# An fp32 attention and two-MoE kernel on Trainium2: the first MoE's last pair in seven products, with low halves of its outputs for two token blocks on GpSimd

## The chip, the core and the metric

The kernel runs on one core of a Trainium2 chip. The metric is the time of one execution on the device in microseconds (us); the matrix engine is TensorE (PE), with PEld for its weight loads, and the others are VectorE (DVE), ScalarE (ACT), GpSimd (POOL) and SyncE (SP), which issues the DMAs.

## What is computed

Attention over 2 batches, 8 heads, 768 positions and head size 64, with a window of 128 and 4 sink positions; its output, as 1536 tokens of width 512, goes through two feed-forward blocks. Cut to what matters:

```python
x = attention(q, k, v).transpose(0, 2, 1, 3).reshape(1536, 512)
g = x @ w_gate                          # 512 x 1536
h = g * sigmoid(g) * (x @ w_val)        # w_val 512 x 1536
x = h @ w_out                           # first MoE, w_out 1536 x 512
h = x @ w_in                            # 512 x 2048
h = maximum(h, 0) + alpha * minimum(h, 0)
out = h @ w_out2                        # second MoE, 2048 x 512
```

All inputs and outputs are fp32.

## The kernel before

**Products.** An fp32 product is made of three on PE: each operand is split into a high half (rounded on ACT, `hh`, `yh`, `wh`) and a low half (operand minus high half, `hl`, `yl`, `wl`), and hi x hi, hi x lo and lo x hi are added up in PSUM. Each matmul is 128 x 128 by 128 x 512. `split_hidden` (L700) makes the two halves of a tile, the low half on DVE; `Stream` does it for weights, which arrive as 64-bit words: `w_m` on ACT (L556), three bit operations on DVE (L591, L594, L597), `wh` on ACT (L600) and `wl` on GpSimd (L606).

**Tiling.** The 1536 tokens are three blocks b = 0, 1, 2 of 512. Four tiles of 128 of the first MoE's inner width go first (`Moe1`), then four pairs of tiles, c = 0 to 3 (`Duo1`), then eight pairs of the second MoE (`Duo2`). A pair has a gate projection, a value projection and outputs. `proj` (L684) is one projection of one block and one tile: 12 matmuls (`ph`). An output (`output`, L1038) is six matmuls (`po`) for one of four column tiles m of one block, with an addition to the accumulator `acc` on DVE (L1048); for the last pair, which completes the first MoE, the sum is split as well (`yh`, `yl`), as the operand of the second MoE.

**Seven products.** Pairs c = 1 and 2, and those of the second MoE from its second on, compute the projections of blocks 0 and 1 in seven products of half size, not eight, in the manner of Strassen and Winograd (`Chain`, L879). Operands are the blocks' quarters (`xh`, `xl`), sums of them made once (`t1` to `t4`, each with halves h and l) and sums of weights (`SUMS`, L660; four 128x256 operations on GpSimd, L574 to L577, then `wh` at L580 and a `wl`). A product (`pa`, `pb`, `pc`, L858) is six matmuls. Products that several results share stay in PSUM and go on; ACT keeps a copy (`u1`, `u2`, L868) and DVE adds it to another product (`plus`, L885). Block 2 has no partner and goes by `proj`. `ORDER7` sets the order of the steps; in it the products with `t4` and `t3` have the numbers 4 and 7, the fourth quarter (`b22`) 3, and block 2's two projections 8 and 9. Pairs c = 0 and c = 3 are plain: each block by `proj`.

**From projections to outputs.** The gate's result goes through Silu on ACT to `sg`; the value's is multiplied with it on DVE (`hid`, L977), and the product is split: `hh` on ACT, `hl` on DVE. Index r is the tile in the pair. An output needs `hh` and `hl` of both.

**Order.** A unit is one pair as a Python generator. At the mark `OUT` its rest is held and run after the next unit's first step, so the next pair's first product stands between a pair's last value product and its outputs. In the plain last pair, blocks 0 and 1 have their outputs behind the next block's first projection and only block 2's are held. The order on each engine is then set by the framework's scheduler, which simulates the program and picks what is ready; what is written under `g.soon()` has priority. Weights go through raw tiles into slots: ten pairs of `wh` and `wl` in `w_p`, and two in `w_p3`, which `back` (L1267) opens when the room of `t3` is closed, here after pair 2's outputs; `st.own` names the weights that may use them.

Of the kernel before, what the change touches and what calls it, by code (L numbers as in the profile page):

```python
# [12 lines left out]
ALU = mybir.AluOpType  # L13
# [7 lines left out]
KD = DM // P  # L21
# [12 lines left out]
CHUNK = 4  # L34
DUO = 2
ORDER7 = (1, 2, 5, 6, 8, 7, 9, 4, 3)
WB = 10
RB = 3
# [460 lines left out]
def big(g, name, parts=(0, 1)):  # L499

    return [half(g.x_p, name) if j in parts else None for j in range(2)]
# [161 lines left out]
def duo1_seq(wg, wv, wo):  # L663

    seq = []
    for f in range(CHUNK, NF1, DUO):
        fs = range(f, f + DUO)
        more = SUMS if CHUNK < f < NF1 - DUO else []
        seq += [(0, wg, x, DOWN, x) for x in fs] + more
        seq += [(0, wv, x, DOWN, NF1 + x) for x in fs] + more  # L670
        seq += [(1, wo, x, DOWN, 2 * NF1 + x) for x in fs]
    return seq
# [26 lines left out]

def split_hidden(nc, hid, hh, hl):  # L700
    nc.scalar.activation(hh, hid, AF.Copy)  # L701
    nc.vector.tensor_tensor(out=hl, in0=hid, in1=hh, op=ALU.subtract)  # L702

# [228 lines left out]
class Duo1(Duo):  # L932
# [48 lines left out]

    def plain(self, w, last):

        pairs, ys = {}, {}
        _, gate, _, value = self.sinks(pairs)
# [11 lines left out]

        def second(b):
            y = [big(self.g, n) for n in ("yh", "yl")] if last else None
            for m in range(KD):  # L1000
                self.output(b, m, w + 2 * DUO, *pairs[b], y)
                yield
            if last:
                self.accs[b][1][1] += 1
                self.put(y, self.accs[b][0])

        yield from first(0, 0, gate)
        for b in range(NPASS):
            if b < NPASS - 1:
                yield from first(b, DUO, value)  # L1010
                yield from first(b + 1, 0, gate)
                yield from second(b)
        yield from first(b, DUO, value)
        yield OUT
        yield from second(b)
        self.st.done(DUO)

    def unit(self, c):
        last = (NF1 - CHUNK) // DUO - 1
        w = self.base + (3 * DUO + (c - 1) * 5 * DUO if c else 0)  # L1020
        if c in (0, last):
            yield from self.plain(w, c == last)
            return
        pairs = self.pairs()
        room_g, gate, room_v, value = self.sinks(pairs)
        for i, room, sink in ((0, room_g, gate), (2 * DUO, room_v, value)):
            chain = self.chain(w + i, self.ops, self.xs[2], room, sink)
            yield from chain.steps(ORDER7)
            chain.done()
        yield OUT  # L1030
        for b in (2, 0, 1):
            for m in range(KD):
                self.output(b, m, w + 4 * DUO, *pairs[b])
                yield
        self.st.done(DUO)

    def output(self, b, m, w, hh, hl, y=None):
# [9 lines left out]
        with self.g.soon():  # L1047
            nc.vector.tensor_tensor(out=av, in0=ps, in1=av, op=ALU.add)  # L1048
            if y:
                split_hidden(nc, av, *(chan(t, m) for t in y))  # L1050

# [109 lines left out]
def fast(nc, tc, ctx, g, lim, alpha, qk, vp, vs, w_gate, w_val, w_out, x2_in, x2_out, out):  # L1161
# [97 lines left out]
    inner = ExitStack()  # L1259
    last = (NF1 - CHUNK) // DUO - 1  # L1260

# [5 lines left out]
    def back():  # L1267
        assert not later
        inner.close()
        add_pool(nc, tc, ctx, g.w_ps, "w_p3", WA, "right")  # L1270
        st.own = range(base - 3 * DUO, len(st.seq))

    later.extend(x for y in d1.sums() for x in (None, y))
    units = [(m1.unit(0, 2), lend)] + [(d1.unit(c), back if c == last - 1 else None) for c in range(last + 1)]
    held = None
# [113 lines left out]
```

## Time and profile before

| | before |
|---|---|
| median of three runs | 667.65 us (667.52 to 668.27) |
| the profiled execution's own time | 667.32 us |
| its span, first to last instruction | 665.6 us |
| mean granted clock of TensorE | 0.983 of full speed |
| PE busy, matmuls | 646.0 us (97%), 3032 |
| DVE busy | 474.8 us (71%) |
| ACT busy | 319.8 us (48%) |
| GpSimd busy | 231.7 us (35%) |

How to read it: the profile is one execution, and its instructions have a start and a duration. Busy shares are means over stages. A matmul's row is 0.39 us long though a new one starts every 0.23 us, since matmuls are pipelined, so PE is counted by starts. In an answer on idle time, "a <- b" says that an engine waited before a for b. Tile names leave out the number of the buffer.

### The profile page before, as it was taken

How to read it: one execution, taken by the hardware profiler on the slowest of the kernel's cores; microseconds unless marked ns; L12 is line 12 of the kernel's file. 1: busy time of each engine (PE TensorE's matmuls, PEld its weight loads, DVE VectorE, ACT ScalarE, POOL GpSimd, SP SyncE). 2: the span in 40 equal slices, each digit the busy share in tenths (PEclk: the TensorE clock that was granted, in tenths of full speed). 3: DMA queues.
4: the chain of work that ended last, by engine and by line, in shares of the span. 5: the costliest groups of instructions: out<-in, count | busy, mean ns of one | idle time of the engine just before them, and what ended most of it. 6: DMA issues, size and time to landing. Idle time of an engine off the chain costs nothing.

```text
span 665.6 us, 8776 instructions
## 1 busy us (share of the span) xinstructions
PE 646.0 (97%) x3032; PEld 507.5 (76%) x3032; DVE 474.8 (71%) x933; ACT 319.8 (48%) x738; POOL 231.7 (35%) x259
## 2 busy tenths in 40 slices
PE   7889899999999999999999999999999999999996
PEld 3557566767788788888888888788888888888885
DVE  6897957355199736667898659858796889787554
ACT  4777755665364523452753345755334342524040
POOL 3557545334213532461333123424344252511000
PEclk8889799999999999999999999999999999999999
DMA  8764444100003303213432120212121303000005
GB/s 272 237 190 141 149 126 158 33 13 1 1 0 111 111 1 94 65 32 95 128 126 96 32 64 32 63 65 64 64 96 32 96 32 96 32 1 0 1 1 194
DMA packets 37204, 52.30 MB, mean 79 GB/s; under 512 B 4384, under 2 KB 28960, under 8 KB 37152
## 3 DMA queue, kind: packets, MB, share of 16 engines
q1 hardware_dynamic: 34944, 51.65, 24.4%
q8 instruction: 26, 0.43, 0.3%
q10 hardware_dynamic: 2208, 0.01, 0.2%
q14 instruction: 26, 0.21, 0.1%
HBM read 48.51 MB, written 3.15 MB: 78 GB/s over the span
## 4 chain that ended last, share of the span: by engine, by line
PE 81%; DVE 8%; ACT 4%; issue 2%; POOL 2%; DMA 1%; SPq 0%; ACTq 0%; POOLq 0%; DVEq 0%
PE pa L858 9%; PE pf L1133 7%; PE pf L1132 7%; PE pf L1131 7%; PE ph L688 6%; PE ph L690 6%; PE ph L689 6%; PE pb L858 4%; PE po L1043 3%; PE po L1044 3%; PE po L1045 3%; PE ps_s L227 3%; PE xp L323 2%; PE pc L858 2%; PE ps_p L282 2%
## 5 line engine op out<-in xcount | busy, mean ns | idle before, releaser
L606 POOL TENSOR_TENSOR wl<-w_m,wh 128x512 fp32r<-128x512 f32 x79 | 112.5, 1428 | 231.0 <-ACT wh L600 216.9
L600 ACT ACTIVATE wh<-w_m 128x512 fp32r<-128x512 f32 x68 | 43.0, 633 | 112.7 <-PE pf L1133 49.1
L701 ACT ACTIVATE hh<-hid 128x512 fp32r<-128x512 f32 x84 | 52.6, 630 | 72.5 <-DVE hid L977 29.7
L702 DVE TENSOR_TENSOR hl<-hid,hh 128x512 fp32r<-128x512 f32 x84 | 65.0, 778 | 16.9 <-ACT hh L701 16.5
L1132 PE MATMUL pf<-wl,hh 128*128 128x512 f32 x192 | 74.6, 392 | 0.0
L1131 PE MATMUL pf<-wh,hh 128*128 128x512 f32 x192 | 74.6, 392 | 0.0
L1138 DVE TENSOR_TENSOR acc<-pf,acc 128x512 f32<-128x512 f32 x84 | 54.6, 686 | 23.0 <-PE pf L1133 23.0
L1133 PE MATMUL pf<-wh,hl 128*128 128x512 f32 x192 | 68.9, 392 | 0.0
L556 ACT ACTIVATE w_m<-w_raw 128x512 f32<-128x512 f32 x68 | 45.9, 675 | 33.7 <-POOL wl L606 24.0
L597 DVE SCALAR_TENSOR_TENSOR w_m<-w_raw,w_m 128x512 uint32<-128x512 uint32 x68 | 58.6, 861 | 1.1
L594 DVE SCALAR_TENSOR_TENSOR w_m<-w_raw,w_m 128x512 int32<-128x512 int32 x68 | 52.3, 768 | 1.2
L688 PE MATMUL ph<-xh,wh 128*128 128x512 f32 x128 | 49.8, 389 | 0.0
L690 PE MATMUL ph<-xh,wl 128*128 128x512 f32 x128 | 49.8, 389 | 0.0
L689 PE MATMUL ph<-xl,wh 128*128 128x512 f32 x128 | 49.8, 389 | 0.0
L591 DVE TENSOR_SCALAR w_m<-w_m 128x512 int32<-128x512 int32 x68 | 36.7, 539 | 16.0 <-ACT w_m L556 15.4
L237 ACT ACTIVATE pr<-ps_s,nb 128x160 f32<-128x160 f32 (+2 forms) x96 | 38.1, 407 | 18.9 <-DVE nb L233 16.2
L1048 DVE TENSOR_TENSOR acc<-po,acc 128x512 f32<-128x512 f32 x48 | 31.8, 686 | 19.4 <-PE po L1045 19.3
L227 PE MATMUL ps_s<-th 64*128 64x288 f32 (+2 forms) x192 | 39.3, 443 | 6.0 <-ACT pr L237 4.5
L1132 PEld LDWEIGHTS pf<-wl,hh 128*128 128x128 f32 x192 | 36.1, 188 | 8.1
L1133 PEld LDWEIGHTS pf<-wh,hl 128*128 128x128 f32 x192 | 36.1, 188 | 8.0
L1131 PEld LDWEIGHTS pf<-wh,hh 128*128 128x128 f32 x192 | 36.1, 188 | 8.0
L1043 PE MATMUL po<-hh,wh 128*128 128x512 f32 x96 | 37.5, 391 | 0.6 <-ACT hh L701 0.6
(212 smaller groups left out, 1518.6 us busy)
## 6 DMA issues: line engine op xcount, KB each, us to landing
w_raw<-in_moe_w_out SPq DMA_DIRECT2D x28, 512.0 KB, 3.3
w_raw<-in_moe_w_in SPq DMA_DIRECT2D x16, 512.0 KB, 4.0
w_raw<-in_moe_w_gate SPq DMA_DIRECT2D x12, 512.0 KB, 4.0
w_raw<-in_moe_w_val SPq DMA_DIRECT2D x12, 512.0 KB, 3.7
th<-in_qk SPq DMA_DIRECT2D x16, 336.0 KB, 3.5
vr<-in_v SPq DMA_DIRECT2D x16, 192.0 KB, 2.9
out<-acc SPq DMA_DIRECT2D x12, 256.0 KB, 2.5
th<-in_qk SPq DMA_DIRECT2D x8, 256.0 KB, 5.4
```

The costliest lines, as they stand in the source:

```text
L227: nc.tensor.matmul(pss[e][:, :first + w], self.th[r, qs], self.th[r, ks], start=True, stop=True)
L597: nc.vector.scalar_tensor_tensor(out=mu, in0=lo.bitcast(U32), scalar=29, in1=mu, op0=ALU.logical_shift_right, op1=ALU.bitwise_or)
L606: eng.tensor_tensor(out=wl, in0=m, in1=wh, op=ALU.subtract)
L688: nc.tensor.matmul(ps, wh[:, c], chan(xh, kk), start=(kk == 0), stop=False)
L689: nc.tensor.matmul(ps, wh[:, c], chan(xl, kk), start=False, stop=False)
L690: nc.tensor.matmul(ps, wl[:, c], chan(xh, kk), start=False, stop=(kk == KD - 1))
L702: nc.vector.tensor_tensor(out=hl, in0=hid, in1=hh, op=ALU.subtract)
L858: self.nc.tensor.matmul(ps, a[:, c], m[:, k], start=(start and k == 0 and y == 0), stop=(k == 1 and y == 2), skip_group_check=True)
L1043: nc.tensor.matmul(ps, wh[:, mc], hh[:, x], start=(x == 0), stop=False)
L1131: nc.tensor.matmul(ps, hh[:, x, ts], wh, start=(x == 0), stop=False)
L1132: nc.tensor.matmul(ps, hh[:, x, ts], wl, start=False, stop=False)
L1133: nc.tensor.matmul(ps, hl[:, x, ts], wh, start=False, stop=(x == DUO - 1))
```

## The change

The last pair of the first MoE (c = 3) now goes in seven products too: its weights get the sums, and its value projection the order `LAST7`, in which the product with `t3` stands earlier and block 2's second projection last. Its outputs aren't held; they follow its value projection at once, in block order 0, 1, 2, and `OUT` stands behind them. `back` runs between the two, and only weights of the second MoE may use `w_p3`. Low halves of the pair's final sums for blocks 0 and 1 (8 of 128x512) are made on GpSimd; those of block 2 stay on DVE. `plain` is left for c = 0 alone.

```diff
--- before.py
+++ after.py
@@ -34,6 +34,7 @@
 CHUNK = 4
 DUO = 2
 ORDER7 = (1, 2, 5, 6, 8, 7, 9, 4, 3)
+LAST7 = (1, 2, 6, 5, 7, 8, 4, 3, 9)
 WB = 10
 RB = 3
 WA = 2
@@ -665,7 +666,7 @@
     seq = []
     for f in range(CHUNK, NF1, DUO):
         fs = range(f, f + DUO)
-        more = SUMS if CHUNK < f < NF1 - DUO else []
+        more = SUMS if f > CHUNK else []
         seq += [(0, wg, x, DOWN, x) for x in fs] + more
         seq += [(0, wv, x, DOWN, NF1 + x) for x in fs] + more
         seq += [(1, wo, x, DOWN, 2 * NF1 + x) for x in fs]
@@ -697,9 +698,9 @@
     return [(pool or g.h_p).tile([P, 2, T], F32R, tag=t, name=t) for t in ("hh", "hl")]
 
 
-def split_hidden(nc, hid, hh, hl):
+def split_hidden(nc, hid, hh, hl, eng=None):
     nc.scalar.activation(hh, hid, AF.Copy)
-    nc.vector.tensor_tensor(out=hl, in0=hid, in1=hh, op=ALU.subtract)
+    (eng or nc.vector).tensor_tensor(out=hl, in0=hid, in1=hh, op=ALU.subtract)
 
 
 class Moe1:
@@ -979,9 +980,9 @@
 
         return room_g, gate, room_v, value
 
-    def plain(self, w, last):
-
-        pairs, ys = {}, {}
+    def plain(self, w):
+
+        pairs = {}
         _, gate, _, value = self.sinks(pairs)
 
         def first(b, i, sink):
@@ -996,43 +997,47 @@
                 yield
 
         def second(b):
+            for m in range(KD):
+                self.output(b, m, w + 2 * DUO, *pairs[b])
+                yield
+
+        yield from first(0, 0, gate)
+        for b in range(NPASS - 1):
+            yield from first(b, DUO, value)
+            yield from first(b + 1, 0, gate)
+            yield from second(b)
+        yield from first(NPASS - 1, DUO, value)
+        yield OUT
+        yield from second(NPASS - 1)
+        self.st.done(DUO)
+
+    def unit(self, c):
+        last = c == (NF1 - CHUNK) // DUO - 1
+        if c == 0:
+            yield from self.plain(self.base)
+            return
+        w = self.base + 3 * DUO + (c - 1) * 5 * DUO
+        pairs = self.pairs()
+        room_g, gate, room_v, value = self.sinks(pairs)
+        for i, room, sink, order in ((0, room_g, gate, ORDER7), (2 * DUO, room_v, value, LAST7 if last else ORDER7)):
+            chain = self.chain(w + i, self.ops, self.xs[2], room, sink)
+            yield from chain.steps(order)
+            chain.done()
+        if last:
+            self.then()
+        else:
+            yield OUT
+        for b in (0, 1, 2) if last else (2, 0, 1):
             y = [big(self.g, n) for n in ("yh", "yl")] if last else None
             for m in range(KD):
-                self.output(b, m, w + 2 * DUO, *pairs[b], y)
+                self.output(b, m, w + 4 * DUO, *pairs[b], y)
                 yield
             if last:
                 self.accs[b][1][1] += 1
                 self.put(y, self.accs[b][0])
-
-        yield from first(0, 0, gate)
-        for b in range(NPASS):
-            if b < NPASS - 1:
-                yield from first(b, DUO, value)
-                yield from first(b + 1, 0, gate)
-                yield from second(b)
-        yield from first(b, DUO, value)
-        yield OUT
-        yield from second(b)
         self.st.done(DUO)
-
-    def unit(self, c):
-        last = (NF1 - CHUNK) // DUO - 1
-        w = self.base + (3 * DUO + (c - 1) * 5 * DUO if c else 0)
-        if c in (0, last):
-            yield from self.plain(w, c == last)
-            return
-        pairs = self.pairs()
-        room_g, gate, room_v, value = self.sinks(pairs)
-        for i, room, sink in ((0, room_g, gate), (2 * DUO, room_v, value)):
-            chain = self.chain(w + i, self.ops, self.xs[2], room, sink)
-            yield from chain.steps(ORDER7)
-            chain.done()
-        yield OUT
-        for b in (2, 0, 1):
-            for m in range(KD):
-                self.output(b, m, w + 4 * DUO, *pairs[b])
-                yield
-        self.st.done(DUO)
+        if last:
+            yield OUT
 
     def output(self, b, m, w, hh, hl, y=None):
         nc, st = self.nc, self.st
@@ -1047,7 +1052,7 @@
         with self.g.soon():
             nc.vector.tensor_tensor(out=av, in0=ps, in1=av, op=ALU.add)
             if y:
-                split_hidden(nc, av, *(chan(t, m) for t in y))
+                split_hidden(nc, av, *(chan(t, m) for t in y), eng=nc.gpsimd if b < NPASS - 1 else None)
 
 
 class Duo2(Duo):
@@ -1257,7 +1262,6 @@
                 decide(nc, g)
 
     inner = ExitStack()
-    last = (NF1 - CHUNK) // DUO - 1
 
     def lend():
         assert g.w_ps.pop()[1] == WA
@@ -1268,10 +1272,11 @@
         assert not later
         inner.close()
         add_pool(nc, tc, ctx, g.w_ps, "w_p3", WA, "right")
-        st.own = range(base - 3 * DUO, len(st.seq))
+        st.own = range(base, len(st.seq))
 
     later.extend(x for y in d1.sums() for x in (None, y))
-    units = [(m1.unit(0, 2), lend)] + [(d1.unit(c), back if c == last - 1 else None) for c in range(last + 1)]
+    d1.then = back
+    units = [(m1.unit(0, 2), lend)] + [(d1.unit(c), None) for c in range((NF1 - CHUNK) // DUO)]
     held = None
     for u, then in units + [(d2.unit(c, ys), None) for c in range(NF2 // DUO)]:
         for x in u:
```

In the order of the changed program lines stand one to five later than before (L858 is L859, L977 is L978, L1043 is L1048, L1048 is L1053). The number behind a tile's name is its buffer. PE has 3020 matmuls.

DVE before, where the plain last pair ends its block 0 and goes on to block 1: additions of outputs (`acc1_1256` is block 0's accumulator) and low halves `yl` alternate.

```order
L597 SCALAR_TENSOR_TENSOR w_m_3788<-w_raw_3560,w_m_3788 128x512
L702 TENSOR_TENSOR hl_3535<-hid_3575,hh_3534 128x512
L1048 TENSOR_TENSOR acc1_1256<-po_3626,acc1_1256 128x512
L1048 TENSOR_TENSOR acc1_1256<-po_3645,acc1_1256 128x512
L702 TENSOR_TENSOR yl_3624<-acc1_1256,yh_3622 128x512
L1048 TENSOR_TENSOR acc1_1256<-po_3656,acc1_1256 128x512
L702 TENSOR_TENSOR yl_3624<-acc1_1256,yh_3622 128x512
L1048 TENSOR_TENSOR acc1_1256<-po_3666,acc1_1256 128x512
L702 TENSOR_TENSOR yl_3625<-acc1_1256,yh_3623 128x512 x2
L977 TENSOR_TENSOR hid_3691<-ph_3678,sg_3593 128x512
```

DVE of the change, where the last pair's value products end and its outputs begin (`hid_3656` and `hid_3714` are block 1's, `hid_3684` block 2's, `hid_3703` block 0's second).

```order
L889 TENSOR_TENSOR hid_3656<-pb_3639,u1_3654 128x512
L978 TENSOR_TENSOR hid_3684<-ph_3671,sg_3543 128x512
L978 TENSOR_TENSOR hid_3656<-hid_3656,sg_3555 128x512
L703 TENSOR_TENSOR hl_3343<-hid_3684,hh_3342 128x512
L703 TENSOR_TENSOR hl_3345<-hid_3656,hh_3344 128x512
L978 TENSOR_TENSOR hid_3703<-pa_3590,sg_3579 128x512
L889 TENSOR_TENSOR hid_3714<-pb_3639,u2_3636 128x512
L592 TENSOR_SCALAR w_m_3862<-w_m_3862 128x512
L978 TENSOR_TENSOR hid_3714<-hid_3714,sg_3587 128x512
L703 TENSOR_TENSOR hl_3341<-hid_3703,hh_3340 128x512
```

The results of all three blocks now come together, with multiplications of two SBUF tiles (`hid_3656`, `hid_3714`) among them, and no `yl`.

PE of the change at the same place: the last three matmuls with the fourth quarter (`xh_89`, `xl_91`), then the outputs of block 0 with its second tile (`hh_3340` with `wh_3513`). Ahead of these rows stand `t3`'s six matmuls, ten output matmuls with block 0's first tile, six with `t4` and three with the fourth quarter.

```order
L859 MATMUL pb_3639<-xh_89,wh_3423 128x512
L859 MATMUL pb_3639<-xl_91,wh_3423 128x512
L859 MATMUL pb_3639<-xh_89,wl_3424 128x512
L1048 MATMUL po_3746<-hh_3340,wh_3513 128x512
L1049 MATMUL po_3746<-hh_3340,wl_3514 128x512
L1048 MATMUL po_3766<-hh_3340,wh_3513 128x512
L1049 MATMUL po_3766<-hh_3340,wl_3514 128x512
```

Behind the last t3 matmul stand 22 matmuls up to the first output of block 0's second tile.

GpSimd before, from the last sums of pair 2 through the plain last pair.

```order
L574 TENSOR_TENSOR w_raw_3532<-w_m_3618 128x256
L606 TENSOR_TENSOR wl_3638<-w_m_3618,wh_3637 128x512
L575 TENSOR_TENSOR w_raw_3532<-w_raw_3532,w_m_3595 128x256
L576 TENSOR_TENSOR w_m_3595<-w_m_3595,w_m_3618 128x256
L577 TENSOR_TENSOR w_m_3595<-w_m_3595,w_raw_3532 128x256
L606 TENSOR_TENSOR wl_3743<-w_raw_3532,wh_3742 128x512
L606 TENSOR_TENSOR wl_3765<-w_m_3595,wh_3764 128x512
L606 TENSOR_TENSOR wl_3845<-w_m_3788,wh_3844 128x512
L606 TENSOR_TENSOR wl_3879<-w_m_3850,wh_3878 128x512
L606 TENSOR_TENSOR wl_3959<-w_m_3914,wh_3958 128x512
```

GpSimd of the change, from the sums of the last pair's value weights on (`wl_3757` and `wl_3778` are the second MoE's first two weights, `acc1_1899` is block 1's accumulator).

```order
L607 TENSOR_TENSOR wl_3778<-w_m_3762,wh_3777 128x512
L577 TENSOR_TENSOR w_m_3719<-w_m_3719,w_m_3762 128x256
L578 TENSOR_TENSOR w_m_3719<-w_m_3719,w_raw_3669 128x256
L607 TENSOR_TENSOR wl_3839<-w_m_3719,wh_3838 128x512
L607 TENSOR_TENSOR wl_3886<-w_m_3862,wh_3885 128x512
L703 TENSOR_TENSOR yl_3744<-acc1_1256,yh_3742 128x512 x2
L703 TENSOR_TENSOR yl_3745<-acc1_1256,yh_3743 128x512 x2
L703 TENSOR_TENSOR yl_3808<-acc1_1899,yh_3806 128x512 x2
L703 TENSOR_TENSOR yl_3809<-acc1_1899,yh_3807 128x512
L607 TENSOR_TENSOR wl_3908<-w_m_3891,wh_3907 128x512
L703 TENSOR_TENSOR yl_3809<-acc1_1899,yh_3807 128x512
L607 TENSOR_TENSOR wl_3965<-w_m_3939,wh_3964 128x512
```

Between the low halves of weights there are now eight low halves of outputs, which DVE had before.

## Rows read from the trace of the kernel before

**Rows 1.** The page, busy us (share of the span) and instructions of each engine.
```profile
PE 646.0 (97%) x3032; PEld 507.5 (76%) x3032; DVE 474.8 (71%) x933; ACT 319.8 (48%) x738; POOL 231.7 (35%) x259
```

**Rows 2.** All waits of PE, 180 to 420 us: total, times, longest.
```profile
PE po L1043 <- ACT hh L701: 0.6, 1, 0.6
```

**Rows 3.** Stages of 20 us: busy us and instructions of each engine, clock, DMA.
```profile
core 0: us, PE busy (x) PEld busy (x) DVE busy (x) ACT busy (x) POOL busy (x), PEclk, DMA share, GB/s
...
340.00:360.00 20.00, 20.00 (x90) 16.58 (x89) 19.33 (x32) 8.37 (x18) 5.72 (x4) 1.00 0.33 106
360.00:380.00 20.00, 20.00 (x90) 16.58 (x89) 13.07 (x20) 7.42 (x13) 5.89 (x6) 1.00 0.17 52
380.00:400.00 20.00, 20.00 (x90) 16.57 (x89) 12.01 (x18) 8.16 (x14) 4.56 (x3) 1.00 0.17 54
400.00:420.00 20.00, 20.00 (x88) 16.24 (x88) 20.00 (x27) 13.75 (x23) 8.79 (x8) 1.00 0.08 27
```

**Rows 4.** Timeline of PE: start, duration, engine, line, operation; 23 rows left out between.
```profile
389.18 0.39 PE L1043 MATMUL po<-hh,wh 128*128 128x512 f32 x1
...
394.62 0.39 PE L688 MATMUL ph<-xh,wh 128*128 128x512 f32 x1
```

**Rows 5.** Timelines of PE, DVE and ACT where pair 0 hands over to its outputs.
```profile
231.77 0.50 PE L1043 MATMUL po<-hh,wh 128*128 128x512 f32 x1 [0.56 <-ACT hh L701]
...
230.37 0.68 DVE L977 TENSOR_TENSOR hid<-ph,sg 128x512 f32<-128x512 f32 x1
...
231.09 0.63 ACT L701 ACTIVATE hh<-hid 128x512 fp32r<-128x512 f32 x1 [1.09 <-DVE hid L977]
```

**Rows 6.** Timelines of PE, DVE and ACT around pair 2's last value products.
```profile
343.39 0.39 PE L858 MATMUL pa<-t4h,wl 128*128 128x512 f32 x1
...
343.82 0.69 DVE L977 TENSOR_TENSOR hid<-pa,sg 128x512 f32<-128x512 f32 x1
...
337.82 0.58 ACT L868 ACTIVATE u<-pa 128x512 f32<-128x512 f32 x1
```

**Rows 7.** Timelines of DVE and POOL at places where both are busy or one is alone.
```profile
346.39 1.78 DVE L977 TENSOR_TENSOR hid<-hid,sg 128x512 f32<-128x512 f32 x1
...
345.83 1.78 POOL L606 TENSOR_TENSOR wl<-w_m,wh 128x512 fp32r<-128x512 f32 x1 [0.23 <-ACT wh L600]
...
353.55 1.88 DVE L1048 TENSOR_TENSOR acc<-po,acc 128x512 f32<-128x512 f32 x3
...
353.78 1.31 POOL L606 TENSOR_TENSOR wl<-w_m,wh 128x512 fp32r<-128x512 f32 x1 [6.17 <-ACT wh L600]
...
389.92 1.29 POOL L606 TENSOR_TENSOR wl<-w_m,wh 128x512 fp32r<-128x512 f32 x1 [1.49 <-ACT wh L580]
...
397.72 1.22 DVE L702 TENSOR_TENSOR t1l<-acc,t1h 128x1024 fp32r<-128x1024 f32 x1
398.85 0.69 DVE L702 TENSOR_TENSOR yl<-acc,yh 128x512 fp32r<-128x512 f32 x1
399.45 0.69 DVE L977 TENSOR_TENSOR hid<-ph,sg 128x512 f32<-128x512 f32 x1
400.05 1.72 DVE L844 TENSOR_TENSOR acc<-acc 128x1024 f32<-128x1024 f32 x1
...
398.02 2.66 POOL L606 TENSOR_TENSOR wl<-w_m,wh 128x512 fp32r<-128x512 f32 x1 [6.81 <-ACT wh L600]
...
406.66 0.42 DVE L591 TENSOR_SCALAR w_m<-w_m 128x512 int32<-128x512 int32 x1
...
411.43 2.08 POOL L606 TENSOR_TENSOR wl<-w_m,wh 128x512 fp32r<-128x512 f32 x1 [7.91 <-ACT wh L600]
```

**Rows 8.** Groups by line and form: line, engine, tile, count, busy us, mean ns, idle before.
```profile
L606 POOL TENSOR_TENSOR wl<-w_m,wh 128x512 fp32r<-128x512 f32 x79 | 112.5, 1428 | 231.0 <-ACT wh L600 216.9 <-PE pf L1133 10.5 <-ACT wh L580 3.0
...
L575 POOL TENSOR_TENSOR w_raw<-w_raw,w_m 128x256 f32<-128x256 f32 x11 | 8.6, 781 | 0.3
```

## The prediction

> **What bounds the kernel now.** Begin with the page's busy shares: TensorE (PE) works 646.0 of 665.6 us [rows 1], so either matmuls leave the program or PE starts to wait. Next come PE's waits. In the MoE part there is one, 0.6 us long, at the hand-off of the first pair to its outputs [rows 2]; from 180 us to the end the matmuls otherwise follow each other without a gap. The stage table shows PE full in every 20 us of the stretch concerned and its clock at 1.00 of full speed, so nothing is hidden in a slow clock; VectorE (DVE) has reserve before 400 us and none from 400 to 420 [rows 3]. DVE therefore bounds nothing on average and is full exactly where the first MoE ends and the second begins. That stretch decides. 24 output matmuls lie between the starts of two rows 5.44 us apart [rows 4]: one matmul costs 0.2267 us of PE, and this pitch is the unit below (the 0.39 us of a row overlaps the next row).
>
> **Fewer matmuls: -2.7 us.** A plain pair is 2 projections x 2 chunks x 3 blocks x 12 = 144 matmuls; in seven products it is 2 x (7 x 6 + 24) = 132. The outputs keep theirs. 12 x 0.2267 = 2.7 us off a full PE.
>
> **What I cost at nothing.** Two sums more for gate and two for value bring GpSimd eight 128x256 operations and four `wl`: with the means of [rows 8] 8 x 0.78 + 4 x 1.43 = 12 us, spread over 340 to 400 us where GpSimd is busy 16 of 60 us [rows 3]. Four more `wh` on ScalarE (ACT) stand in the same stretch, where ACT is under half busy. If that cover were gone, a late weight would stop PE for up to one conversion. DVE gets six additions of a product to a kept sum and loses eight low halves. SP's transfers keep their order, and no DMA is added. The weight slots are those with which pairs 1 and 2 run without a wait [rows 2], ten of them, the two of `w_p3` coming one pair later.
>
> **The new hand-off: +2.3 us (0.5 to 3.0).** Before, the last pair is plain and its blocks' outputs alternate with the next block's projections, so nothing has to be ready at once. After seven products nothing may be held back here, because the second MoE needs all outputs. PE's order has, after the last t3 matmul, 10 output matmuls, 6 with t4 and 6 with the fourth operand: 22, then the first output of block 0 that needs its second hidden chunk. From the start of the last t3 matmul that is 23 x 0.2267 = 5.2 us. What must be done by then, walked through in DVE's and ACT's order from the start of that matmul (0):
> - ACT keeps the product: a consumer starts 0.43 after a matmul's start (343.39 to 343.82), it takes 0.58 [rows 6], so it ends at 1.0.
> - DVE adds it to `pb` (1.1 to 1.7) and multiplies block 2's `ph` (1.7 to 2.3). Both read PSUM. Back to back a 512-wide instruction costs 0.60, from three in 1.88 us where one alone takes 0.68 [rows 7].
> - The multiplication `hid<-hid,sg` reads SBUF twice. In [rows 7] such an instruction at 346.39 took 1.78 us beside a `wl` on GpSimd that had begun at 345.83, where DVE's normal time is 0.68. The `wl` of the second MoE's first weight becomes ready just here (1.7 to 3.0 at 1.29 us), so the multiplication goes from 3.0 to 3.6.
> - `hl` of block 2 (3.6 to 4.2). DVE then waits for ACT's `hh`, and in that gap GpSimd takes the next `wl` (4.2 to 5.5); `hl` of block 1 follows until 6.1.
> - Only then comes `hid<-pa` (6.1 to 6.8), ACT's `hh` (0.63, to 7.4) and PE at 7.5.
>
> 7.5 - 5.2 = 2.3 us of waiting. Without the second `wl` in the gap the chain is 1.3 shorter (1.0); the nearest row is the old hand-off of pair 0, where DVE finished `hid` and ACT began 0.72 us after DVE's start, and PE lost 0.56 [rows 5]: lower end 0.5. One more stretched instruction gives 3.0.
>
> **Low halves on GpSimd: +1.9 us (0 to 7.1).** The rows show how DVE and GpSimd share. A `wl` alone takes 1.29 us (389.92). Beside DVE instructions with both inputs in SBUF it took 2.08 (411.43) and 2.66 (398.02), and DVE's `acc<-acc` behind it 1.72 instead of 1.22; the three `acc<-po` at 353.55, with an input in PSUM, ran undisturbed at 0.60 beside a `wl` of 1.31 [rows 7]. So SBUF-only work of the two engines adds up, and PSUM work does not. The Trainium skill, "SBUF — State Buffer", "Who interferes with whom", states this as a rule: a DVE instruction with two SBUF inputs and a GpSimd instruction that reads SBUF lock each other out for the whole instruction; by it the move frees no time at all, as GpSimd holds the shared ports for longer than DVE would. The trace agrees (1.78, 2.66, 1.72). If the two engines ran side by side instead, this term would be 0.
>
> From the first output of block 0's second chunk to the matmul that needs block 1's last low half PE has 96 matmuls: 21.8 us. In that stretch GpSimd has eight low halves and three `wl`, 11 x 1.29 = 14.2 us. DVE's SBUF-only instructions there are ten 512 wide (10 x 0.60), two 1024 wide (2 x 1.13, the distance from 397.72 to 398.85) and three bit operations (3 x 0.42) [rows 7]: 9.5 us. 23.7 - 21.8 = 1.9 us. Lower end 0: the first low half can begin some 5 us after the stretch begins, and nine GpSimd instructions in the remaining 16.7 us fit at 1.29 (11.6). At 2.08 each they need 18.7, which is 2.0 too long and close to my value; at 2.66 each 23.9, the upper end of 7.1. I take 1.9 because DVE is busy without pause here before as well, so undisturbed times are the exception.
>
> **Block 2's low halves on DVE: +1.0 us (0 to 2.6).** They stand behind everything above. From block 0's first outputs to the matmul that reads the last of them are 122 matmuls, 27.7 us. DVE has about 22.7 us of work up to that instruction, GpSimd 12 x 1.29 = 15.5; of the 38.2 us some 8 can lie beside each other (DVE's 13 additions from PSUM, 0.60 each), leaving 30.2: 2.5 us over, of which 1.9 is already counted; rounded up for ACT's `yh` in between, 1.0. Lower end 0 if the gaps fall well; upper end two GpSimd instructions in the way, 2.6.
>
> **Sum.** -2.7 + 2.3 + 1.9 + 1.0 = +2.5 us on the profiled execution's 667.3: 669.8. The median of the runs shown is 0.33 higher, so I forecast **670.1**.
>
> **The rivals.**
> 1. *All hidden (faster, on the other side).* For it: PE has hardly waited in 480 us, the scheduler placed `t3` early so that 22 matmuls cover the chain, and GpSimd is two thirds idle. Against it: [rows 7]. The place is the hand-off: if the two `wl` come late enough to miss DVE's gaps, PE loses 1.0 there or less, and if GpSimd's instructions fit at 1.29 the low halves cost nothing. It decides at a total loss under 1.4 us. Time: 667.65 - 2.7 + 0.5 to 1.4 = 665.4 to 666.3.
> 2. *Hand-off only (no change).* The stall of 2 to 3 us is there, the low halves arrive in time: 667.65 - 2.7 + 2.3 = 667.2, with its bounds 666.4 to 668.0. For it: PE reads block 0's low halves only 50 matmuls (11.3 us) after that block's last output matmul. Against it: DVE is 20.00 of 20 us busy at 400 to 420 even before [rows 3].
> 3. *GpSimd starved (much slower).* Each low half waits behind a train of DVE instructions as at 398.02: the term is 7.1 instead of 1.9, and block 2's term falls into it: 667.65 - 2.7 + 2.3 + 7.1 = 674.4; from 672 up. Against it: DVE's additions from PSUM stand between the SBUF-only ones and let GpSimd in.
>
> That the twelve matmuls do not go is no rival: PE's order has 3020.
>
> **How the numbers follow.** Chances: forecast (two or three of the costs, 668.9 to 672) 0.40; all hidden 0.27; hand-off only 0.20; starved 0.13. A measurement of this kernel tells about 0.2% (1.3 us) from no change: below 666.3 is faster, above 669.0 slower. So faster 0.27, same 0.20, slower 0.40 + 0.13 = 0.53. The likeliest case's own range is 668.9 to 672. For 8 in 10 I reach down to 665.2, just under the all-hidden case with the smallest hand-off, and up to 672.8; beyond lie most of the starved case and little else.
>
> **What would show it.** Of the profile after: 3020 matmuls; among PE's waits one of about 2.3 us, on ACT's `hh`, at the first output of block 0's second chunk; in the timeline of DVE there, SBUF-only instructions of 1 us and more beside a `wl`; low halves on GpSimd with a mean of 1.6 to 2.1 us; PE waits on GpSimd's `yl` of 1 to 2 us in the second MoE's first products and one on DVE's `yl`. PE without a wait over 0.6 us would make my forecast wrong, as would a wait for a weight. If the waits are there but fall together elsewhere, the terms are wrong and the mechanism may stand.

## The result and the profile after

The changed kernel takes 672.74 us (672.06 to 673.13, five runs) where the kernel before, run beside it, takes 667.52: a ratio of 1.0077, 95% interval 1.0063 to 1.0091, so 5.2 us slower. The forecast was 670.1, slower, range 665.2 to 672.8: the result lies 0.06 us inside the range and above the likeliest case's own 668.9 to 672. The profiled execution took 673.06 us, 5.74 more than the one of before.

The page's busy shares after:

```profile
PE 645.0 (96%) x3020; PEld 504.7 (75%) x3020; DVE 477.8 (71%) x931; ACT 324.9 (48%) x748; POOL 255.9 (38%) x279
```

The 12 matmuls are gone, and DVE's busy time rose by 3.0 us though it has two instructions less. Against [rows 2], the waits of PE after the first pair's hand-off (235 us to the end):

```profile
PE po L1048 <- ACT hh L702: 2.2, 1, 2.2
PE pa L859 <- ACT u L869: 1.4, 1, 1.4
PE pf L1136 <- DVE hid L1094: 0.9, 1, 0.9
PE pf L1138 <- DVE hl L703: 0.4, 1, 0.4
PE ph L690 <- DVE yl L703: 0.3, 1, 0.3
```

None waits on GpSimd directly. Before, the same stretch had no wait. The stages of 20 us, with the columns of [rows 3]:

```profile
380.00:400.00 20.00, 17.77 (x71) 13.86 (x70) 16.42 (x22) 10.28 (x20) 11.91 (x10) 0.91 0.26 79
400.00:420.00 20.00, 20.00 (x90) 16.55 (x89) 20.00 (x23) 9.99 (x17) 16.15 (x10) 1.00 0.17 53
420.00:440.00 20.00, 16.87 (x69) 12.03 (x68) 16.86 (x22) 13.58 (x24) 9.52 (x7) 1.00 0.09 27
```

Time is lost in two places, and between them PE is full while DVE never pauses (20.00 of 20) and GpSimd works 16 us instead of 9. PE's timeline through the first place:

```profile
384.20 0.39 PE L859 MATMUL pa<-t3h,wl 128*128 128x512 f32 x1
...
389.20 0.39 PE L859 MATMUL pb<-xh,wl 128*128 128x512 f32 x1
391.82 0.50 PE L1048 MATMUL po<-hh,wh 128*128 128x512 f32 x1 [2.23 <-ACT hh L702]
...
393.47 0.63 PE L1048 MATMUL po<-hh,wh 128*128 128x512 f32 x1
393.89 0.63 PE L1049 MATMUL po<-hh,wl 128*128 128x512 f32 x1
...
396.62 0.39 PE L1049 MATMUL po<-hh,wl 128*128 128x512 f32 x1
```

From the start of the last t3 matmul the hand-off takes 391.82 - 384.20 = 7.6 us. From 393.5 us most matmuls start 0.42 to 0.43 us apart, not 0.2267: the clock is at its lower level, and the windows show when:

```profile
389.00:393.00 4.00, 1.77 (x8) 1.17 (x7) 4.00 (x7) 2.24 (x5) 2.72 (x3) 1.00 0.13 24
393.00:396.30 3.30, 3.30 (x10) 2.20 (x9) 3.30 (x5) 1.71 (x4) 0.78 (x1) 0.52 0.37 130
396.30:400.00 3.70, 3.70 (x17) 3.10 (x16) 3.70 (x6) 2.79 (x6) 2.46 (x2) 0.97 0.46 140
```

DVE and GpSimd during the hand-off:

```profile
386.46 1.21 DVE L978 TENSOR_TENSOR hid<-hid,sg 128x512 f32<-128x512 f32 x1
387.59 2.91 DVE L703 TENSOR_TENSOR hl<-hid,hh 128x512 fp32r<-128x512 f32 x2
390.43 0.68 DVE L978 TENSOR_TENSOR hid<-pa,sg 128x512 f32<-128x512 f32 x1
...
387.08 1.74 POOL L607 TENSOR_TENSOR wl<-w_m,wh 128x512 fp32r<-128x512 f32 x1
388.78 1.18 POOL L577 TENSOR_TENSOR w_m<-w_m 128x256 f32<-128x256 f32 x1
```

From 386.46 to 390.43 DVE needs 3.97 us for three instructions that cost 0.60 each back to back: 2.2 us of stretching, which is the size of the wait. GpSimd's two `wl` and its sum in this stretch belong to one pair of weights of the second MoE, neither to its first two weights nor to the last pair's value weights, as the part on the change has them: the low half of this pair's second sum is begun at 392.37, when the last value product (389.20) has long started. The low halves on GpSimd (number, min/median/max in ns, first and last start):

```profile
L703 POOL TENSOR_TENSOR yl<-acc,yh x8: 1486/1742/2269, 398.8 to 412.2; 128x512 fp32r<-128x512 f32 x8
```

And the second place, in the second MoE's first pairs; DVE, ACT, GpSimd and PE:

```profile
428.04 1.22 DVE L703 TENSOR_TENSOR t4l<-acc,t4h 128x1024 fp32r<-128x1024 f32 x1
429.17 1.28 DVE L1094 TENSOR_TENSOR hid<-ph,neg 128x512 f32<-128x512 f32 x2
433.49 1.59 DVE L703 TENSOR_TENSOR hl<-hid,hh 128x512 fp32r<-128x512 f32 x1 [3.03 <-ACT hh L702]
...
431.82 0.63 ACT L581 ACTIVATE wh<-w_raw 128x512 fp32r<-128x512 f32 x1 [4.78 <-POOL w_raw L576]
432.36 0.58 ACT L869 ACTIVATE u<-pa 128x512 f32<-128x512 f32 x1
432.84 0.62 ACT L702 ACTIVATE hh<-hid 128x512 fp32r<-128x512 f32 x1
...
426.52 3.34 POOL L575 TENSOR_TENSOR w_raw<-w_m 128x256 f32<-128x256 f32 x1 [10.37 <-PE pa L859]
431.06 0.73 POOL L576 TENSOR_TENSOR w_raw<-w_raw,w_m 128x256 f32<-128x256 f32 x1
...
425.58 0.39 PE L1136 MATMUL pf<-wh,hh 128*128 128x512 f32 x1
...
432.99 0.50 PE L859 MATMUL pa<-t2h,wh 128*128 128x512 f32 x1 [1.42 <-ACT u L869]
...
439.17 0.50 PE L1136 MATMUL pf<-wh,hh 128*128 128x512 f32 x1 [0.91 <-DVE hid L1094]
```

Block 1's first product of the second MoE ended at 416 us by the count of matmuls; DVE reads it 13 us later, at 429.17. From there the engines hold each other up in turn. GpSimd's first operation of a weight sum takes 3.34 us, where such an operation takes 0.73 alone (431.06): it ends at 429.86, 0.69 us after DVE has gone from instructions with two SBUF inputs to this `hid`, which reads PSUM. The next operation of the sum follows at 431.06. ACT's queue stands 4.78 us for it, with `u` and block 1's `hh` behind: both `hid` of block 1 are done at 430.45, and the first `hh` begins at 432.84. For `hh` DVE in turn is idle for 3.03 us, and PE waits for `u`, `hl` and the next `hid`.

Below, PE's **loss** in a stretch is the sum of what neighbouring starts lie further apart than 0.2267 us, where they are over 0.25 apart. After: 4.2 us from 380 to 400 (2.4 the wait, 0.1 the next matmul, 1.7 the slow clock) and 4.7 from 420 to 441 (0.55 at 421, 4.1 from 429 to 440). Less the 12 matmuls and the 0.2 us that before loses: 8.9 - 2.7 - 0.2 = 6.0, against 5.74 measured.

### The profile page after: what moved, and what is told of

It is laid out like the page before. It is cut to its first block, busy times and chain, and to the rows that moved or that the text cites. A ratio compares the mean times of both kernels' runs of the same rounds, so it can differ in the third digit from the quotient of the medians.

```text
span 671.3 us, 8799 instructions
## 1 busy us (share of the span) xinstructions
PE 645.0 (96%) x3020; PEld 504.7 (75%) x3020; DVE 477.8 (71%) x931; ACT 324.9 (48%) x748; POOL 255.9 (38%) x279
## 4 chain that ended last, share of the span: by engine, by line
PE 73%; DVE 13%; issue 5%; ACT 4%; POOL 2%; DMA 1%; SPq 0%; POOLq 0%; DVEq 0%; ACTq 0%
PE pa L859 10%; PE pf L1136 6%; PE pf L1137 6%; PE pf L1138 6%; PE pb L859 5%; PE ph L691 4%; PE ph L690 4%; PE ph L689 4%; PE pc L859 3%; PE po L1048 2%; PE po L1049 2%; PE po L1050 2%; PE xp L324 2%; DVE w_m L595 2%; PE ps_s L228 2%
## 5 line engine op out<-in xcount | busy, mean ns | idle before, releaser
L703 DVE TENSOR_TENSOR hl<-hid,hh 128x512 fp32r<-128x512 f32 x84 | 66.8, 801 | 20.8 <-ACT hh L702 20.4
L1136 PE MATMUL pf<-wh,hh 128*128 128x512 f32 x192 | 73.2, 392 | 1.0 <-DVE hid L1094 0.9
L598 DVE SCALAR_TENSOR_TENSOR w_m<-w_raw,w_m 128x512 uint32<-128x512 uint32 x68 | 56.8, 835 | 1.0
L1048 PE MATMUL po<-hh,wh 128*128 128x512 f32 x96 | 38.0, 396 | 2.8 <-ACT hh L702 2.8
L1053 DVE TENSOR_TENSOR acc<-po,acc 128x512 f32<-128x512 f32 x48 | 31.5, 683 | 12.5 <-PE po L1050 12.5
L1049 PE MATMUL po<-hh,wl 128*128 128x512 f32 x96 | 37.8, 394 | 0.0
L691 PE MATMUL ph<-xh,wl 128*128 128x512 f32 x96 | 37.4, 389 | 0.0
L690 PE MATMUL ph<-xl,wh 128*128 128x512 f32 x96 | 37.3, 389 | 0.0
```

Of the source, the lines that this page charges most:

```text
L598: nc.vector.scalar_tensor_tensor(out=mu, in0=lo.bitcast(U32), scalar=29, in1=mu, op0=ALU.logical_shift_right, op1=ALU.bitwise_or)
L690: nc.tensor.matmul(ps, wh[:, c], chan(xl, kk), start=False, stop=False)
L691: nc.tensor.matmul(ps, wl[:, c], chan(xh, kk), start=False, stop=(kk == KD - 1))
L703: (eng or nc.vector).tensor_tensor(out=hl, in0=hid, in1=hh, op=ALU.subtract)
L1136: nc.tensor.matmul(ps, hh[:, x, ts], wh, start=(x == 0), stop=False)
```

## The experiments

| version | time, us | ratio to before (95%) | loss 380-400 | 400-420 | 420-441 |
|---|---|---|---|---|---|
| the change | 672.74 | 1.0077 (1.0063 to 1.0091) | 4.2 | 0 | 4.7 |
| 1 low halves all on DVE | 667.63 | 1.0010 (0.9999 to 1.0021) | 3.2 | 0 | 0.1 |
| 2 before, low halves on GpSimd | 668.97 | 1.0022 (1.0005 to 1.0039) | 0 | 1.6 | 0 |
| 3 low halves as copies on ACT | 667.81 | 1.0009 (1.0000 to 1.0019) | 4.1 | 0 | 0 |
| 4 half of them on GpSimd | 672.02 | 1.0066 (1.0046 to 1.0086) | 3.3 | 0 | 5.3 |
| 5 one ACT instruction moved | 671.90 | 1.0070 (1.0044 to 1.0095) | 4.1 | 0 | 4.2 |
| 6 outputs 2, 0, 1 | 671.43 | 1.0068 (1.0050 to 1.0087) | 0.3 | 2.3 | 5.9 |
| 7 the same, DVE | 670.77 | 1.0052 (1.0032 to 1.0071) | 0.3 | 6.8 | 0.2 |
| 8 the same, second MoE too | 669.45 | 1.0022 (1.0013 to 1.0031) | 0.1 | 0.3 | 4.4 |
| 9 no weights at the hand-off | 672.51 | 1.0071 (1.0047 to 1.0095) | 4.3 | 0.8 | 2.3 |
| 10 block 2 last | 667.98 | 1.0003 (0.9993 to 1.0012) | 1.9 | 0.6 | 1.1 |
| 11 the same, one `hl` on GpSimd | 672.70 | 1.0076 (1.0058 to 1.0094) | 5.4 | 0 | 1.3 |
| 12 as 10, copies on ACT | 667.27 | 0.9999 (0.9987 to 1.0011) | 1.7 | 1.2 | 0 |

Times of before in the four later groups of runs: 667.44, 667.43, 667.68 and 667.36. The losses are those of one profiled execution each; less the 2.7 and the 0.2 us they give the difference of the medians to 1.6 us. The profiled execution can lie off its median: in version 10 it took 665.97 us, in 11 670.83 and in 4 673.42.

One thing holds for all versions: the scheduler orders the engines anew for each, so a version can change more than its edit. Where that bears on a result, it is said.

### Low halves on GpSimd: undone, alone, left out, halved

**1. All on DVE.**

```diff
-                split_hidden(nc, av, *(chan(t, m) for t in y), eng=nc.gpsimd if b < NPASS - 1 else None)
+                split_hidden(nc, av, *(chan(t, m) for t in y), eng=None)
```

> The change with all low halves of the final sums on DVE, as before; the seven products, their order and the outputs' order stay. Theory A (port lock): the eight low halves on GpSimd and DVE's instructions with two SBUF inputs shut each other out; GpSimd's took 12.2 us for seven where DVE needs about 4.2, so DVE falls behind with the bit operations of the second MoE's weights, and PE's losses from 421 to 440 us (4.8 us over the pitch) come from there. It expects these losses to fall to 0 to 2 us and 668 to 670 us. Theory B (bunching): the losses come from the results of three blocks arriving together, whoever splits them; with 4.8 us more for DVE they stay or grow: 672 to 677 us. Both leave the hand-off (2.5 us) and what follows it as they are.

Measured: 5.1 us faster than the change. PE's waits from 235 us:

```profile
PE po L1048 <- ACT hh L702: 2.2, 1, 2.2
PE po L1050 <- DVE hl L703: 0.5, 1, 0.5
```

The hand-off stays, the second place is gone. B's 672 to 677 is ruled out; A's loss (0 to 2) comes out, and the time is 0.4 us under its 668 to 670. But PE's order is another one too: its outputs of the second MoE's first pair begin here at 420.59, and in the change at 425.58, behind all 72 products of that pair. Run 1 therefore doesn't tell the move from the order that came with it.

```profile
420.59 0.39 PE L1136 MATMUL pf<-wh,hh 128*128 128x512 f32 x1
```

**2. The kernel before with this part alone** (`eng` as in the change, last pair plain).

> The kernel before with one part of the change alone: low halves of the final sums of blocks 0 and 1 on GpSimd, the last pair plain. Theory A expects a loss here too, 1 to 4 us (668.5 to 671.5), as DVE is full from 400 to 420 us already. Theory B expects nothing (667.0 to 668.2): in the plain pair the blocks' results come one after the other and GpSimd has room.

Measured: +1.5 us, inside A's range, by one wait of 1.3 us at an output, where DVE's 1024-wide instructions are stretched beside the low halves:

```profile
398.66 2.34 DVE L702 TENSOR_TENSOR t1l<-acc,t1h 128x1024 fp32r<-128x1024 f32 x1
400.92 2.31 DVE L844 TENSOR_TENSOR acc<-acc 128x1024 f32<-128x1024 f32 x1
...
398.63 3.52 POOL L702 TENSOR_TENSOR yl<-acc,yh 128x512 fp32r<-128x512 f32 x2 [2.78 <-ACT yh L701]
```

The 1.22 us of `t1l` in [rows 7] became 2.34. So the move costs time without seven products, less than with them.

**3. No subtraction for the two blocks.**

```diff
-    (eng or nc.vector).tensor_tensor(out=hl, in0=hid, in1=hh, op=ALU.subtract)
+    if eng:
+        nc.scalar.activation(hl, hid, AF.Copy)
+    else:
+        nc.vector.tensor_tensor(out=hl, in0=hid, in1=hh, op=ALU.subtract)
```

The copies are no low halves, so this version measures what the subtractions cost and doesn't compute the product.

> The change, but ACT writes the low halves of blocks 0 and 1 as plain copies: the subtraction for these two blocks is left out, and with it every use of the ports that GpSimd and DVE share. ACT is half idle there. Theory A expects the losses from 421 to 440 us to go and the hand-off to stay: 667.5 to 669.0. Theory B expects 671 to 673: the bunching of DVE's other work is the same.

Measured: A's time, and no loss behind the hand-off. DVE's first additions after the hand-off, and its reading of block 1's first product with `t4l`, in the change, in 1 and in 3:

```profile
396.65 1.28 DVE L1053 TENSOR_TENSOR acc<-po,acc 128x512 f32<-128x512 f32 x2
```
```profile
396.80 1.28 DVE L1053 TENSOR_TENSOR acc<-po,acc 128x512 f32<-128x512 f32 x2
...
428.12 1.28 DVE L1094 TENSOR_TENSOR hid<-ph,neg 128x512 f32<-128x512 f32 x2
429.32 1.39 DVE L703 TENSOR_TENSOR t4l<-acc,t4h 128x1024 fp32r<-128x1024 f32 x1
```
```profile
396.73 1.27 DVE L1056 TENSOR_TENSOR acc<-po,acc 128x512 f32<-128x512 f32 x2
...
423.24 1.22 DVE L706 TENSOR_TENSOR t4l<-acc,t4h 128x1024 fp32r<-128x1024 f32 x1
424.37 1.28 DVE L1097 TENSOR_TENSOR hid<-ph,neg 128x512 f32<-128x512 f32 x2
```

This is the plainest measure of the move. From those additions to the end of both `hid` and `t4l`, DVE has the same 40 instructions in the change and in run 3, and these with the eight low halves in run 1. They take 28.9 us in run 3, 33.9 in run 1 and 33.8 in the change. So the eight cost DVE 5.0 us when it makes them itself (8 x 0.60 = 4.8) and 4.9 us when GpSimd makes them: the move frees nothing. (That `hid` starts 1.1 us later in the change than in run 1 is order: `t4l` stands ahead of it there and behind it in run 1.)

It also shows that DVE is as late in run 1 as in the change, and run 1 loses nothing. PE's order in the change is close to that of run 3, where its first output comes at 425.01 behind all 72 products, and there DVE is 4.9 us earlier. So the change pairs an order that goes well with DVE free of the eight low halves with a DVE that isn't free of them. That this pairing is what costs the time is the reading that fits the three profiles; no run held the order fixed.

**4. Four on GpSimd** (`if b == 0`).

> The change with the low halves of block 0 alone on GpSimd (4 of 8), those of blocks 1 and 2 on DVE. If the backlog grows with each instruction on GpSimd, half of the loss from 420 to 441 us stays: 2 to 2.7 us, 669.5 to 670.5 in all. If there is slack first, so that only the last few low halves push the weights past their time, the loss is 0 to 1 us: 667.5 to 668.7.

Measured: neither case. Half of the low halves lose about as much as all, in other waits (1.9 us on ACT's `hh` at 431.5 and slow matmuls behind it). ACT's queue again stands for the sum, with `hh` behind:

```profile
432.63 0.63 ACT L581 ACTIVATE wh<-w_raw 128x512 fp32r<-128x512 f32 x1 [3.58 <-POOL w_raw L576]
```

So the loss is no sum over instructions: it depends on what stands behind the late sum.

**5. ACT's queue.** In the change ACT stands 4.8 us before a weight's high half that waits for GpSimd's sum, with `u` behind it. Here that instruction alone is on GpSimd.

```diff
-            nc.scalar.activation(wh, m, AF.Copy)
+            if self.alone == i:
+                nc.gpsimd.tensor_copy(out=wh, in_=m)
+            else:
+                nc.scalar.activation(wh, m, AF.Copy)
...
+    st.alone = base + 6 * DUO
```

> The change with one instruction elsewhere: the high half of the weights' first sum for the second MoE's pair 2 is made on GpSimd, behind the sum itself, not on ACT. In the trace of the change ACT's queue stands still in front of it from 427.0 to 431.8 us, with the kept product (u) that PE waits for behind it. If that place in ACT's queue turns GpSimd's lateness into PE's waits, the losses from 420 to 441 us fall from 4.6 to 0.5 to 1.5 us, and the time to 668.5 to 669.8, with all eight low halves still on GpSimd. If DVE's own lateness with the hidden values is what PE waits for, the losses stay above 3 us: 671 to 673.

Measured: the second case's numbers; the loss is 4.2. PE no longer waits for `u`, but for what stood behind:

```profile
PE pf L1139 <- DVE hid L1097: 0.9, 1, 0.9
PE pf L1139 <- ACT hh L705: 0.8, 1, 0.8
PE pf L1141 <- DVE hl L706: 0.7, 1, 0.7
```

That isn't DVE's lateness alone. ACT's queue stands again, now in front of the next weight's `w_m`, which waits for another operation of the same sums, and the second `hh` of block 1 follows only at 432.31, though its `hid` was done at 429.0:

```profile
431.64 0.66 ACT L557 ACTIVATE w_m<-w_raw 128x512 f32<-128x512 f32 x1 [1.98 <-POOL w_m L577]
```

The edit took one place out of ACT's queue and another took over, so this run doesn't decide between ACT's place and DVE's lateness.

### The hand-off

**6. Outputs in order 2, 0, 1** with `ORDER7`; the three results are handed on in order 0, 1, 2 as before.

```diff
-        for b in (0, 1, 2) if last else (2, 0, 1):
+        late = []
+        for b in (2, 0, 1):
...
-                self.put(y, self.accs[b][0])
+                late.append((y, self.accs[b][0]))
...
```

> The change with the last pair's outputs in block order 2, 0, 1 and the step order of the other pairs; low halves of blocks 0 and 1 stay on GpSimd. Block 2's hidden values are ready early, so 45 matmuls instead of 22 stand between the last t3 matmul and the first output of block 0's second tile: 10.2 us against a chain of 7.6. If the hand-off's wait (2.4 us) is the chain alone and the slow stretch behind it (1.7 us at half the clock) is that wait's consequence, both go: about 668.5 with the later losses unchanged. If the slow stretch comes without a wait too, it stays and the time is about 670.

Measured: the wait and the slow clock both go (0.3 us of 4.2), as expected, but the time falls by 1.3, not 4.2. PE reaches the second MoE earlier and waits there, 0.6 us on a low half from GpSimd, 2.1 on `hl`, at half the clock afterwards. Blocks 0 and 1, which the second MoE reads first, are now last.

**7. The same with low halves on DVE.**

> Both repairs together: outputs of the last pair in block order 2, 0, 1 with the step order of the other pairs, and all low halves of the final sums on DVE. If the two losses are independent, the hand-off costs 0.3 us (as with the block order alone), 421 to 441 us costs nothing (as with DVE's low halves alone), and the 12 matmuls' 2.7 us come through: 665.0 to 665.6 us. If block 0's and block 1's low halves, now the last on DVE, come too late for the second MoE's first products, PE waits 1 to 2.5 us there: 666 to 667.5.

Measured: both expectations fail; worse than 1. One wait takes it back, with 13 slow matmuls behind it:

```profile
PE ph L689 <- ACT yh L702: 3.5, 1, 3.5
```

**8. Block 2 first in the second MoE too**, low halves on DVE as in 7.

```diff
-            for b in range(NPASS):
+            for b in (2, 0, 1):
                 pairs[b] = hidden_pair(self.g, self.g.h_p2 if b == 1 else None)
...
-        for b in (2, 0, 1) if c else range(NPASS):
+        for b in (2, 0, 1):
             yield from self.outputs(c, b, w, *pairs[b])
```

> Block order 2, 0, 1 for the last pair's outputs and for the second MoE's first pair too, all low halves on DVE. With the order 2, 0, 1 in the last pair alone PE waited 3.5 us for block 0's results at the second MoE's first product and then ran 13 matmuls at half the clock. Now block 2, finished first, is also read first: its 24 products (5.4 us) cover that wait. If the wait was only the order in which blocks are read, hand-off and later losses are 0.3 and under 1 us: 664.8 to 665.8. If DVE is late for all blocks alike, PE waits 2 us or more further on: 667 to 669.

Measured: the hand-off and the wait of 3.5 us are gone, and 4.4 us are lost at 427 to 434 instead (2.4 on `hh`, 1.4 on `hid`). That is the loss of the second expectation, at a time 0.45 us over its 669, but not for its reason. The `hid` in question was done at 426.6; its `hh` stood in ACT's queue behind a `wh` that waited for GpSimd's sum, as in the change, here with all low halves on DVE:

```profile
428.94 0.63 ACT L581 ACTIVATE wh<-w_raw 128x512 fp32r<-128x512 f32 x1 [3.59 <-POOL w_raw L576]
430.14 0.50 PE L1139 MATMUL pf<-wh,hh 128*128 128x512 f32 x1 [2.43 <-ACT hh L702]
```

**9. No weights during the last four value steps** (`st.tick()` held back there and made up later; low halves on DVE).

> The change with all low halves on DVE, and no weight converted during the last four steps of the last pair's value products (they follow later, two at a time), so that no wl of GpSimd falls into the hand-off. If the two wl hold up DVE's multiplication and low half there, the wait of PE falls from 2.23 to 0.5 to 1.3 us, and the time from 667.6 to 666.0 to 667.0. If the chain is bound by DVE's own instructions, the wait stays at 1.8 to 2.3 us and the time at 667.4 to 668.

Measured: inconclusive. The wait is 2.4 us, but GpSimd again had two `wl` there (of other weights, 385.54 to 388.54), and two bit operations stood in DVE's queue ahead of the low half. The edit did not remove what it was meant to.

**10. Block 2's value projections last**, low halves on DVE.

```diff
-LAST7 = (1, 2, 6, 5, 7, 8, 4, 3, 9)
+LAST7 = (1, 2, 6, 5, 7, 4, 3, 8, 9)
```

> The change with all low halves on DVE and block 2's projections last in the value chain's steps (order 1, 2, 6, 5, 7, 4, 3, 8, 9). On DVE block 2's multiplication and low half then stand behind block 0's second multiplication, on which the hand-off waits: 1.2 us of five instructions leave the chain, and with the shorter chain one of the places where GpSimd's wl can come between. If the hand-off is DVE's chain with GpSimd between, PE's wait there falls from 2.23 to 0.3 to 1.1 us: 665.3 to 666.6 in all. If PE waits for something else (the kept product on ACT, the weights), it stays at 2 us and the time at 667.4 to 668.

Measured: PE's wait falls to 1.1 us, the upper end for a DVE chain, with no slow clock. The time, 668.0, misses the 665.3 to 666.6: it is that of before. The profile has 1.7 us lost behind the hand-off.

**11. One low half less on DVE there.** `split_hidden` of block 1's second tile takes `eng=nc.gpsimd` in the last unit.

> The version with block 2's projections last and the final low halves on DVE, with one low half at the hand-off (hidden values of block 1's second tile) on GpSimd: it stood on DVE right ahead of block 0's second multiplication, for which PE waited 1.1 us; on GpSimd it falls behind the two wl, and its first reader comes 20 matmuls after the hand-off. If that chain is DVE's, the wait falls to 0 to 0.4 us and the time to 0.6 to 1.2 us under that version: 666.2 to 667.2 where the kernel before has 667.5. If the wait moves into the low half on GpSimd, which must take its turn with DVE, the sum of the two waits stays at 1 us or more: 667.5 to 668.5.

Measured: the wait at block 0's output is 0.1, and block 1's output waits instead, 3.1 us on `hh` of its other tile. DVE's multiplication for that came at 394.35, after four others, one of them a bit operation of 1.51 us beside GpSimd's low half:

```profile
390.63 1.51 DVE L592 TENSOR_SCALAR w_m<-w_m 128x512 int32<-128x512 int32 x1
...
394.35 0.68 DVE L979 TENSOR_TENSOR hid<-hid,sg 128x512 f32<-128x512 f32 x1
```

With one low half on GpSimd, and the order that the scheduler chose for it, this version is 4.7 us slower than 10; both expectations (666.2 to 668.5) fail.

**12. As 10, without the subtraction for blocks 0 and 1** (edit of 3).

> The version with block 2's projections last, but ACT writes the low halves of blocks 0 and 1 of the final sums as plain copies: the subtraction for these two blocks is left out, and DVE has eight instructions less, with nothing more for GpSimd. If what holds PE there now is DVE's and GpSimd's common work, the losses behind the hand-off (1.7 us in that version's profile) go and the matmuls' 2.7 us come through but for the hand-off's 1.5: 666.0 to 666.8. If something else holds PE, the time stays at 667.5 to 668.

Measured: as fast as before, and by the ratios 0.3 us faster than 10 (within their intervals), where 1.2 us or more were expected. The time lies between the two cases. The loss from 420 us is gone, but a wait of 0.9 us on `hh` at 418 and the hand-off's 1.1 remain. So even with eight DVE instructions left out the 12 matmuls aren't seen in the time.

## Why the prediction was right, and where not

The number lies inside the range by luck: two terms were short by 3.9 us together, and the range ends 0.06 us above the result. By time it would be rival 3 (from 672 up), but the low halves weren't starved as that rival has it: they took 1.74 us (median), 2.27 at most.

- **12 matmuls, 2.7 us:** right, 3020 matmuls and an unchanged pitch. In no version did they come through: each loses as much again or more.
- **What I cost at nothing:** right. No wait for a weight at the last pair, none on SP.
- **The hand-off, 2.3 us:** right in size (2.4), place, length of the chain (7.6 us for 7.5) and mechanism by the rows: SBUF-only instructions on DVE stretched beside GpSimd, three of them where two were forecast, the third beside a sum and not in a gap of DVE's. That GpSimd makes the whole of it rests on those rows; run 9, meant to show it, did not. That the wait is the chain, run 10 shows (1.1 with fewer instructions in it), and that it can be covered, run 6.
- **What the wait does to the clock, 1.7 us:** missing. I called the clock of the stretch 1.00 and costed a wait as its own length.
- **Low halves on GpSimd, 1.9 us (0 to 7.1):** that the two engines' SBUF-only work adds up was right, the place wrong and the size too small. The instructions took 1.74 us (median), and no matmul waited for one of them. The step that failed is the 96 matmuls to block 1's last low half as the point where the two engines' common time comes due. It came due some 20 us later: 4.1 us, on `u`, `hl` and `hid`, by way of a late sum on GpSimd and ACT's queue behind it. Run 1 takes it away by undoing the move, run 2 has a smaller loss with the move alone, and run 3 shows DVE 4.9 us earlier without the eight; in each the order changes too, in run 3 least. The Trainium skill, "SBUF — State Buffer", "Who interferes with whom", says that a DVE instruction with two SBUF inputs contends with a GpSimd instruction that reads SBUF, and that the lock is exclusive. The trace agrees: the same 40 instructions of DVE take 33.8 us beside GpSimd's low halves and 28.9 without them.
- **Block 2's low halves, 1.0 us:** 0.55, at 421 us, on DVE's `yl` as described.
- **The sum:** 2.4 + 0.1 + 1.7 + 0.55 + 4.1 - 2.7 - 0.2 = 6.0 (5.74 between the two executions, 5.2 between the medians) for a forecast of 2.5. The rival "hand-off only" is what run 1 is: 667.6 for 667.2.

No version here beats the kernel before by more than its measurement can tell. Version 10 equals it.

What stays open: why the same wait of 2.2 us was followed by the lower clock in the change and in runs 3 and 5, but not in 1 and 4; how much of the second place's 4.1 us is the order and how much the common time of DVE and GpSimd; and the same for the remaining loss in version 10. A version with GpSimd silent at the hand-off was not reached.

## What to carry to other kernels

Work with both inputs in SBUF that is moved from DVE to GpSimd doesn't leave DVE where GpSimd takes twice as long for it and the two exclude each other: count such instructions of both engines as one queue. Where a stage is held by that queue, matmuls saved on PE can come back as waits: here no version with 3020 matmuls lost less than the 2.7 us that were saved. When a profile names several small waits behind each other, follow each back through the queues before repairing the first one. Here DVE held up GpSimd, a sum on GpSimd held up ACT's queue, and what stood behind in that queue held up DVE and PE; with one place in the queue repaired, the next took over.

## What was not expected of the hardware

Behind a wait PE can run at its lower clock level (1.2 of 2.4 GHz, matmuls 0.43 us apart) for 3 to 6 us, beginning up to 1.3 us after it resumed. After waits of 3.5 us (run 7), 3.1 us (run 11) and 2.1 us (run 6) it did so; after one of 2.23 us in three of five profiles; after 2.4 us in runs 8 and 9 not. In run 7, from 406 to 412 us:

```profile
406.00:412.00 6.00, 5.23 (x12) 4.13 (x13) 6.00 (x11) 3.79 (x7) 1.04 (x2) 0.50 0.21 82
```

That cost 2.8 us on top of the 3.5. And the time of the kernel before goes with its mean clock: 665.5 us at 0.990 and 669.2 at 0.978 in one group of runs.

A GpSimd instruction can wait through a whole train of DVE instructions with two SBUF inputs. The first operation of the sum ends 0.67 to 0.69 us after DVE starts the PSUM-reading `hid` behind that train in six profiles (the change and runs 1, 3, 4, 5 and 8), whether it had begun 1.0 or 2.7 us before.
